# Strassen's seven block products for the second MLP's products with w_a and w_b

## The chip, the cores and the metric

The kernel runs on one core of a Trainium2 chip. The metric is the device time of one execution in microseconds, as the median of several runs. Beside it there is one profiled execution, from which all rows here are taken.

## The reference

Sparse attention (a window and block summaries) makes x of 1536 tokens by 512. Two MLPs follow; the change is in the second one. All data are float32; the weights come in as float64, which the kernel turns to float32 words itself.

```python
h = x @ w_in                        # 512 -> 2048
x = (h * sigmoid(h)) @ w_out        # 2048 -> 512, the y of the kernel
a = x @ w_a                         # 512 -> 1536
b = x @ w_b                         # 512 -> 1536
out = (a * b) @ w_out2              # 1536 -> 512
```

## The kernel before

Every float32 product is made of three passes of TensorE: each operand is split into a high part (a cast to fp32r) and a low part (the rest), and high by high, high by low and low by high are added up in PSUM (`PARTS`). The high part is a copy on ScalarE (ACT), the low part a subtraction on GpSimd (POOL) or VectorE (DVE). A matmul covers 128 rows of the contraction, 128 weight columns and 512 tokens.

A 128x512 piece of weights is loaded as 512 KB of words (`load_words`, L440), decoded by a scaled activation on ACT, a shift (L464) and a join (L468) on DVE, and split (`split`, L493: the high part at L144, the low part on POOL at L491). What is needed for each block of 512 tokens again, w_out and the second MLP's w_out2, is spilled to DRAM as float32 (`spill`) and read back (`reload`).

The first part of the program (attention and the start of the first MLP) is written out as the list `ORDER`. The first MLP then runs in 48 slots, three blocks of 512 tokens by 16 pieces: in slot i the matmuls of `mm1(i)` (L514) and of `mm2(i - 2)` (L545), twelve each. From slot 28 on the loop also loads, decodes and splits one piece of w_a or w_b per slot, which all stay in SBUF.

The last part is the second MLP: 36 jobs, three token blocks by twelve column pieces. In job j `mm34(j, "a")` and `mm34(j, "b")` (L574) make twelve matmuls each into a PSUM bank of their own, two banks each in turn; `chain2(j)` copies a (ACT, L584), multiplies (DVE, L589), takes the high part (ACT, L590) and the low part (DVE, L591); then `mm5(j - 1, t)` adds the job before it to the outputs of four groups of 128 tokens (L601), twelve matmuls. In the first twelve jobs pieces of w_out2 are decoded too.

Every engine works through its instructions in the order in which the program gives them out (`tc.manual_schedule()`), and waits for semaphores at their head. All DMAs go through SP's queue.

Of the kernel before, what the change touches and what calls it, by code (L numbers as in the profile page):

```python
# [18 lines left out]
P = 128  # L19
# [62 lines left out]
def attention_then_two_mlps(ctx, tc, q, k, v, w_in, w_out, w_a, w_b, w_out2, out):  # L82
# [19 lines left out]
    N2 = F2 // P  # L102
    NSTEP = B * NJ
# [18 lines left out]
    boot = ExitStack()  # L122
    ps_b = boot.enter_context(tc.tile_pool(name="ps_b", bufs=1, space=PSUM))
# [316 lines left out]
    def load_words(kind, f, pool):  # L440
        t = pool.tile([P, TB, 2], U32, tag="stage", name=f"st_{kind}{f}", bufs=STAGE_BUFS)
# [9 lines left out]
    def decode_a(kind, f):  # L451
# [3 lines left out]
        w32 = w32_t[kind, f] = work.tile([P, TB], F32, tag="w32", name=f"w32_{kind}{f}", bufs=3)  # L455
# [81 lines left out]
    def mm2(i):  # L537
        n, f = divmod(i, N1)
        g, w = g_t.pop(i), wout_t.pop(i)
        if f == 0:  # L540
            for c in range(NK):
                y_ps[n, c] = pools["y"].tile([P, TB], F32, tag=f"y{c}", name=f"y{n}_{c}", bufs=1)
        for c in range(NK):
            for a, m in PARTS:
                nc.tensor.matmul(y_ps[n, c], w[:, a, c * P:(c + 1) * P], g[:, m, :],  # L545
                                 start=(f == 0 and (a, m) == (0, 0)),
                                 stop=(f == N1 - 1 and (a, m) == PARTS[-1]))
        if f == N1 - 1:
            if n:
                for c in range(NK):  # L550
                    y_high(n, c)
                    y_low(n, c)

    def y_high(n, c):
        if n not in y_t:
            y_t[n] = x_pools[n].tile([P, 2, NK, TB], F32R, tag="xy", name=f"yt{n}", bufs=2 if n < 2 else 1)
        nc.scalar.copy(y_t[n][:, 0, c, :], y_ps[n, c])

    def y_low(n, c):
        y = y_t[n]  # L560
        nc.vector.tensor_tensor(y[:, 1, c, :], y_ps[n, c], y[:, 0, c, :].bitcast(F32), op=ALU.subtract)


    JOBS = NBLK * N2
    wab_t, wo2_t, p_t, ab_ps, o_ps = {}, {}, {}, {}, {}

    def mm34(j, which):
        n, f = divmod(j, N2)
        pool = pools["h"] if which == "a" else pools["g"]
        ps = pool.tile([P, TB], F32, tag="h", name=f"{which}{j}")  # L570
        idx = 0
        for c in range(NK):
            for a, m in PARTS:
                nc.tensor.matmul(ps, wab_t[which, f][:, a, c * P:(c + 1) * P], y_t[n][:, m, c, :],  # L574
                                 start=(idx == 0), stop=(idx == 3 * NK - 1))
                idx += 1
        ab_ps[which, j] = ps

    def chain2(j):

        pa, pb = ab_ps.pop(("a", j)), ab_ps.pop(("b", j))
        sg = work.tile([P, TB], F32, tag="sg", name=f"a_sb{j}")
        g = work.tile([P, 2, TB], F32R, tag="g", name=f"p{j}", bufs=3)
        nc.scalar.copy(sg, pa)  # L584
        parts = 2 if j == JOBS - 1 else 1
        ab = sg if j == JOBS - 1 else pb
        for i in range(parts):
            c = slice(i * TB // parts, (i + 1) * TB // parts)
            nc.vector.tensor_tensor(ab[:, c], pb[:, c], sg[:, c], op=ALU.mult)  # L589
            nc.scalar.copy(g[:, 0, c], ab[:, c])  # L590
            nc.vector.tensor_tensor(g[:, 1, c], ab[:, c], g[:, 0, c].bitcast(F32), op=ALU.subtract)  # L591
        p_t[j] = g

    def mm5(j, t):

        n, f = divmod(j, N2)
        g, w = p_t[j], wo2_t[j]
        if f == 0:
            o_ps[n, t] = pools["y"].tile([P, DM], F32, tag=f"y{t}", name=f"o{n}_{t}", bufs=1)
        for a, m in PARTS:  # L600
            nc.tensor.matmul(o_ps[n, t], g[:, a, t * P:(t + 1) * P], w[:, m],  # L601
                             start=(f == 0 and (a, m) == (0, 0)),
                             stop=(f == N2 - 1 and (a, m) == PARTS[-1]))
        if f == N2 - 1:
# [12 lines left out]
    with tc.manual_schedule():  # L617
# [30 lines left out]
        def end_first():  # L648
            first.close()
            pools["x2"] = x_pools[2] = ctx.enter_context(tc.tile_pool(name="x2", bufs=1, side="right"))  # L650

        def end_att():
            att.close()
            pools["late"] = ctx.enter_context(tc.tile_pool(name="late", bufs=1))
# [23 lines left out]
            "m1": mm1, "sg": silu, "gh": gate_high, "gl": gate_low, "m2": mm2, "yh": y_high, "yl": y_low,  # L678
# [19 lines left out]
        for i in range(att_end + 1, SLOTS):  # L698
# [6 lines left out]
            if i < att_end + 2 * N2:  # L705
                w34(i - att_end, pools["late"])
# [79 lines left out]
```

## Time and profile before

| | |
|---|---|
| Median of 3 runs | 652.96 us (651.45 to 653.8) |
| Profiled execution | 651.7 us, of which the instructions span 650.0 us |
| TensorE's granted clock | 0.999 of full speed |
| PE busy | 632.3 us, 97% of the span |
| DVE, ACT, POOL busy | 314.9, 297.2, 225.4 us |
| Last part (products with w_a, w_b and w_out2) | from 345.77 us to the end |

The engines run side by side, so the busy times don't add up. An engine's busy time tells how much work it has; the chain of waits tells which work the end waits for.

### The profile page before, as it was taken

Reading aid. Unit: us, or ns where it says so; the run is one execution under the profiler, and the core shown is the slowest. Engines: PE = TensorE matmul, PEld = TensorE weight load, DVE = VectorE, ACT = ScalarE, POOL = GpSimd, SP = SyncE. Lnnn points to the kernel's source line nnn. Section 1 sums busy time; section 2 is a strip of 40 time slices with the busy share of each in tenths; the row PEclk is TensorE's granted clock in tenths of the full one; section 3 lists DMA queues with packets and bytes.
Section 4 is the critical chain, followed back from the end, with each engine's and each line's share of the span. In section 5 each row is a group of like instructions: output and inputs, shape, how many; then the busy total and the mean of one; then the engine's idle time right before and its main releaser. Section 6 shows DMA issues by size and latency. Waiting matters only on the chain.

```text
span 650.0 us, 9031 instructions
## 1 busy us (share of the span) xinstructions
PE 632.3 (97%) x3296; PEld 524.2 (81%) x3296; DVE 314.9 (48%) x631; ACT 297.2 (46%) x644; POOL 225.4 (35%) x197
## 2 busy tenths in 40 slices
PE   6899999899999999999999999999999999999997
PEld 5888877788878888888888888888888888888886
DVE  6999878985753244544445664442111112211112
ACT  4999678858655125655555342222222222221112
POOL 5657566553233315455553331111111111111111
PEclk9999999999999999999999999999999999999999
DMA  9898997754121234344453432221311110311101
GB/s 232 182 225 254 287 268 244 200 167 114 47 70 49 59 102 141 131 150 143 145 189 113 172 109 98 97 82 32 114 33 33 33 32 17 113 33 32 33 18 65
DMA packets 80148, 75.72 MB, mean 117 GB/s; under 512 B 37848, under 2 KB 62680, under 8 KB 80104
## 3 DMA queue, kind: packets, MB, share of 16 engines
q1 hardware_dynamic: 80104, 75.15, 39.6%
q8 instruction: 26, 0.43, 0.3%
q14 instruction: 18, 0.15, 0.1%
HBM read 64.36 MB, written 10.49 MB: 115 GB/s over the span
## 4 chain that ended last, share of the span: by engine, by line
PE 83%; ACT 6%; DVE 6%; DMA 2%; issue 2%; SPq 0%; DVEq 0%; ACTq 0%
PE y L545 17%; PE h L514 16%; PE o L601 15%; PE a L574 15%; PE b L574 15%; DMA sp_out<-w_out 2%; PE sc L357 2%; ACT sm L386 1%; PE av L420 1%; PE pt L406 1%; DVE u_in L464 1%; ACT qb L345 1%; DVE w_in L468 1%; DVE raw_q L146 1%; DMA st_q<-in_q_dram 1%
## 5 line engine op out<-in xcount | busy, mean ns | idle before, releaser
L514 PE MATMUL h<-x,w_in 128*128 128x512 f32 (+1 forms) x612 | 142.3, 382 | 0.8 <-DVE g L529 0.6
L545 PE MATMUL y<-g,w_out 128*128 128x512 f32 x576 | 140.9, 394 | 0.7 <-DVE w_out L491 0.7
L491 POOL TENSOR_TENSOR w_out<-re_out,w_out 128x512 fp32r<-128x512 f32 x49 | 68.0, 1389 | 206.0 <-ACT w_out L144 198.7
L514 PEld LDWEIGHTS h<-x,w_in 128*128 128x128 f32 x612 | 108.9, 188 | 22.9 <-issue 0.8
L545 PEld LDWEIGHTS y<-g,w_out 128*128 128x128 f32 x576 | 106.8, 188 | 24.2 <-DVE w_out L491 1.2
L589 DVE TENSOR_TENSOR b<-b,a_sb 128x512 f32<-128x512 f32 x35 | 24.5, 700 | 174.2 <-PE b L574 174.2
L574 PE MATMUL a<-yt,w_a 128*128 128x512 f32 x432 | 104.3, 390 | 0.0
L601 PE MATMUL o<-w_out,p 128*128 128x512 f32 x432 | 104.2, 390 | 0.0
L574 PE MATMUL b<-yt,w_b 128*128 128x512 f32 x432 | 104.1, 390 | 0.0
L601 PEld LDWEIGHTS o<-w_out,p 128*128 128x128 f32 x432 | 81.1, 188 | 17.4
L574 PEld LDWEIGHTS a<-yt,w_a 128*128 128x128 f32 x432 | 81.1, 188 | 17.3
L574 PEld LDWEIGHTS b<-yt,w_b 128*128 128x128 f32 x432 | 81.1, 188 | 17.1
L584 ACT COPY a_sb<-a 128x512 f32<-128x512 f32 x36 | 21.1, 585 | 107.3 <-PE a L574 107.3
L590 ACT CAST p<-b 128x512 fp32r<-128x512 f32 x35 | 20.5, 586 | 101.5 <-DVE b L589 101.5
L491 POOL TENSOR_TENSOR w_out<-w_out,w_out 128x512 fp32r<-128x512 f32 x23 | 30.9, 1343 | 90.2 <-ACT w_out L144 81.7
L529 DVE TENSOR_TENSOR g<-h,g 128x512 fp32r<-128x512 f32 x31 | 21.4, 691 | 66.1 <-ACT g L144 66.0
L529 POOL TENSOR_TENSOR g<-sg,g 128x512 fp32r<-128x512 f32 x17 | 24.4, 1438 | 36.7 <-ACT g L144 13.5
L591 DVE TENSOR_TENSOR p<-b,p 128x512 fp32r<-128x512 f32 x35 | 24.2, 691 | 22.8 <-ACT p L590 22.8
L144 ACT CAST w_out<-re_out 128x512 fp32r<-128x512 f32 x50 | 31.1, 623 | 7.6 <-PE y L545 5.1
L522 ACT ACTIVATE h<-h 128x512 f32<-128x512 f32 x31 | 18.0, 582 | 29.6 <-PE h L514 29.6
L464 DVE TENSOR_SCALAR u_out<-st_out 128x512 uint32<-128x512 uint32 x28 | 29.1, 1044 | 0.0
L386 ACT ACTIVATE sm<-sm,st 128x120 f32<-128x120 f32 x76 | 29.1, 390 | 0.1
(119 smaller groups left out, 706.7 us busy)
## 6 DMA issues: line engine op xcount, KB each, us to landing
st_out<-in_moe_w_out_dram SPq DMA_DIRECT2D x28, 512.0 KB, 4.3
re_out<-sp_out SPq DMA_DIRECT2D x56, 256.0 KB, 2.7
st_in<-in_moe_w_in_dram SPq DMA_DIRECT2D x16, 512.0 KB, 5.8
sp_out<-w_out SPq DMA_DIRECT2D x28, 256.0 KB, 2.3
st_a<-in_moe_w_a_dram SPq DMA_DIRECT2D x12, 512.0 KB, 3.7
st_b<-in_moe_w_b_dram SPq DMA_DIRECT2D x12, 512.0 KB
vw<-in_v_dram SPq DMA_DIRECT2D x20, 192.0 KB, 4.1
vg<-in_v_dram SPq DMA_DIRECT2D x8, 384.0 KB, 5.9
```

The costliest lines, as they stand in the source:

```text
L144: nc.scalar.copy(o, i)
L386: nc.scalar.activation(sm[:, pr, :], sm[:, pr, :], AF.Exp, scale=-1.0, bias=st[:, 0, pr:pr + 1], accum_out=st[:, 1, pr:pr + 1])
L464: nc.vector.tensor_scalar(u, t[:, :, 0], 29, None, op0=ALU.logical_shift_right)
L491: engine.tensor_tensor(w[:, 1], w32_t[kind, f], w[:, 0].bitcast(F32), op=ALU.subtract)
L514: nc.tensor.matmul(h_ps[i][:, cols], win_t[f][:, a, c * P:(c + 1) * P], x_t[n][:, steps, m, c, :], start=(idx == 0), stop=(idx == 3 * NK - 1))
L529: engines[engine].tensor_tensor(g_t[i][:, 1], sg_t.pop(i), g_t[i][:, 0].bitcast(F32), op=ALU.subtract)
L545: nc.tensor.matmul(y_ps[n, c], w[:, a, c * P:(c + 1) * P], g[:, m, :], start=(f == 0 and (a, m) == (0, 0)), stop=(f == N1 - 1 and (a, m) = ...
L574: nc.tensor.matmul(ps, wab_t[which, f][:, a, c * P:(c + 1) * P], y_t[n][:, m, c, :], start=(idx == 0), stop=(idx == 3 * NK - 1))
L584: nc.scalar.copy(sg, pa)
L589: nc.vector.tensor_tensor(ab[:, c], pb[:, c], sg[:, c], op=ALU.mult)
L591: nc.vector.tensor_tensor(g[:, 1, c], ab[:, c], g[:, 0, c].bitcast(F32), op=ALU.subtract)
L601: nc.tensor.matmul(o_ps[n, t], g[:, a, t * P:(t + 1) * P], w[:, m], start=(f == 0 and (a, m) == (0, 0)), stop=(f == N2 - 1 and (a, m) == P ...
```

## The change

Per pair of column pieces (128 columns each of two halves of the 1536) and per half of the contraction (two times 256), the 2x2 block product W^T y is done by a form of Strassen's algorithm with seven block products. The 1536 tokens go in two passes of 768, each in two halves of 384, so that a block of y is 256 by 384. One unit is the a or the b of one pair of column pieces (`KINDS`): even units are a, odd ones b, twelve units a pass. A unit has seven products of six matmuls (two times 128 rows by three parts), on 384 tokens. They go into two PSUM banks, A and B, by turns; several products add to what a bank holds after DVE or ACT has read it, and the four results of a unit are made from the banks and three temporaries (t1, u2, u3). After each product k come a `chunk` on PE (one output step of the pair before: three matmuls of 512 columns, in `mm5`) and `fills` on the other engines.

The fills of unit u prepare the weights of unit u + 1: four additions of 128x256 on DVE make the sums S1 to S4 in `c32`, the seven slots are split in `wab` (high parts on ACT in three pieces; low parts on POOL for slots 0 to 2 and 5 to 6, on DVE for 3 to 4). The weights of w_a and w_b no longer stay split in SBUF: the decoded float32 words are spilled (`spill_u`) and a unit of them, 512 KB, is read back two units ahead (`reload_unit`). y is kept as float32 (`keep_y`), its sums T1 to T4 and its seven operands' splits are made for pass one in slots 35 to 47, for pass two in units 2 to 5 (`sums_again`, POOL) and 11 (`split_again`). Four tiles of w_a and w_b are decoded in units 1, 3, 5 and 7, the pieces of w_out2 in the even units of pass one.

```diff
+    PRODUCTS = ((A11, "B11", 0, False), (S2, "T2", 1, False), (A12, "B21", 0, True), (S3, "T3", 1, True),
+                (S1, "T1", 0, False), (A22, "T4", 1, True), (S4, "B22", 0, True))
...
+    def reload_unit(u):
+        open_unit(u)
+        nc.sync.dma_start(c32_t[u][:, 0:4].rearrange("p b x -> p (b x)"), spill_u[u % UNITS].rearrange("p i x -> p (i x)"))
+
+    def prepare(u):
...
+        def lo(e, lo, hi_):
+            return lambda: engines[e].tensor_tensor(wab_t[u][:, 1, lo:hi_], c32_t[u][:, lo + 1:hi_ + 1],
+                                                    wab_t[u][:, 0, lo:hi_].bitcast(F32), op=ALU.subtract)
+        return [hi(0, 3), add("v", 4, 0, 1, ALU.add), lo("p", 0, 3), add("v", 5, 4, 2, ALU.subtract), hi(3, 5),
+                add("v", 6, 2, 0, ALU.subtract), lo("v", 3, 5), add("v", 7, 3, 5, ALU.subtract), hi(5, 7),
+                lo("p", 5, 7)]
...
+    def group(u, chunks, fills, later):
...
+        done = {2: ((0, 0), A, None), 4: ((1, 1), A, u3), 5: ((1, 0), B, t1), 6: ((0, 1), A, u2)}
+        for k, (s, y, b, more) in enumerate(PRODUCTS):
+            ps = (A, B)[b]
+            idx = 0
+            for c in range(2):
+                for a, m in PARTS:
+                    nc.tensor.matmul(ps, W[:, a, s, c * P:(c + 1) * P], yc_t[y][m][:, c, :], start=(idx == 0 and not more),
+                                     stop=(idx == 5), skip_group_check=more)
+                    idx += 1
+            now, later[:] = list(later), []
+            if k == 0:
+                nc.scalar.copy(t1, A)
+            elif k == 1:
+                nc.vector.tensor_tensor(u2, B, t1, op=ALU.add)
+            elif k == 3:
+                nc.vector.tensor_tensor(u3, B, t1, op=ALU.add)
+            else:
+                (i, t), ps, x = done[k]
+                if w == 0:
+                    a_t[i, t] = temp("a", f"a{p}_{i}{t}", 4)
+                    if x is None:
+                        nc.scalar.copy(a_t[i, t], ps)
+                    else:
+                        nc.vector.tensor_tensor(a_t[i, t], ps, x, op=ALU.add)
+                else:
+                    at = a_t[i, t]
+                    hi, lo = high_low_p(p, i, t, "v" if k in (4, 6) else "p")
+                    if x is None:
+                        nc.vector.tensor_tensor(at, ps, at, op=ALU.mult)
+                    else:
+                        ct = temp("c", f"c{p}_{i}{t}", 2)
+                        nc.vector.tensor_tensor(ct, ps, x, op=ALU.add)
+                        engines["v" if k == 6 else "p"].tensor_tensor(at, ct, at, op=ALU.mult)
+                    later.append(lambda hi=hi, lo=lo: (hi(), later.append(lo)))
+            for f in now:
+                f()
+            for f in chunks[k]:
+                f()
+            for f in fills[k]:
+                f()
...
+            if 0 < u < 2 * UNITS - 1:
+                spread(prepare(u + 1))
+            if w == 0:
+                if p < PAIRS:
+                    spread([lambda: decode("out2", 2 * p, pools["w"]), lambda: decode("out2", 2 * p + 1, pools["w"])], 1, 5)
...
+                fills[0].append(lambda p=p: high_wo2(2 * p))
+                fills[1].append(lambda p=p: low_wo2(2 * p))
+                fills[3].append(lambda p=p: high_wo2(2 * p + 1))
+                fills[4].append(lambda p=p: low_wo2(2 * p + 1))
...
+                n = 4 if p == PAIRS else 6
```

How the change moves the instructions on DVE is seen in one pair of jobs before, here jobs 5 and 6 (b and a_sb are the two products, p the result, u_out2 and w32_out2 the decoder's words).

```order
L589 TENSOR_TENSOR b5_3930<-b5_3930,a_sb5_3943 128x512
L591 TENSOR_TENSOR p5_3944<-b5_3930,p5_3944 128x512
L464 TENSOR_SCALAR u_out26_3969<-st_out26_3908 128x512
L468 SCALAR_TENSOR_TENSOR w32_out26_3966<-w32_out26_3966,u_out26_3969 128x512
L589 TENSOR_TENSOR b6_3986<-b6_3986,a_sb6_3999 128x512
L591 TENSOR_TENSOR p6_4000<-b6_3986,p6_4000 128x512
```

After the change this is the stretch of unit 4, the a of pair 2 in pass one, from its product 1 to its end (bank0 and bank1 are the PSUM banks, c32_5 and wab5 the next unit's weights, a2_.. the unit's results).

```order
L468 TENSOR_SCALAR u_out24_4054<-st_out24_3920 128x512
L472 SCALAR_TENSOR_TENSOR w32_out24_4051<-w32_out24_4051,u_out24_4054 128x512
L628 TENSOR_TENSOR c32_5_3915<-c32_5_3915 128x256
L701 TENSOR_TENSOR u3_4_4020<-bank1_3586,t1_4_4018 128x384
L628 TENSOR_TENSOR c32_5_3915<-c32_5_3915 128x256
L468 TENSOR_SCALAR u_out25_4085<-st_out25_3935 128x512
L472 SCALAR_TENSOR_TENSOR w32_out25_4082<-w32_out25_4082,u_out25_4085 128x512
L709 TENSOR_TENSOR a2_11_4096<-bank0_3585,u3_4_4020 128x384
L638 TENSOR_TENSOR wab5_4036<-c32_5_3915,wab5_4036 128x512
L628 TENSOR_TENSOR c32_5_3915<-c32_5_3915 128x256
L709 TENSOR_TENSOR a2_10_4109<-bank1_3586,t1_4_4018 128x384
L709 TENSOR_TENSOR a2_01_4121<-bank0_3585,u2_4_4019 128x384
```

The decoder's rows now stand between readings of PSUM banks (u3, a2_11, a2_10, a2_01), and additions and a low part of weights stand among them, which before was POOL's.

POOL before has nothing but the low parts of weights, here around the start of the last part.

```order
L491 TENSOR_TENSOR w_out20_3647<-w32_out20_3611,w_out20_3647 128x512
L491 TENSOR_TENSOR w_out21_3693<-w32_out21_3654,w_out21_3693 128x512
L491 TENSOR_TENSOR w_b10_3701<-w32_b10_3696,w_b10_3701 128x512
L491 TENSOR_TENSOR w_out22_3763<-w32_out22_3724,w_out22_3763 128x512
L491 TENSOR_TENSOR w_a11_3771<-w32_a11_3766,w_a11_3771 128x512
```

After the change these are POOL's rows of unit 5, the b of pair 2 in pass one (t32 are sums of y, a2_11 and a2_10 the products a * b, p2_00 a low part for the output product; w_out24 and w_out25 are pieces 4 and 5 of w_out2).

```order
L638 TENSOR_TENSOR wab6_4139<-c32_6_4034,wab6_4139 128x768
L495 TENSOR_TENSOR w_out24_4144<-w32_out24_4051,w_out24_4144 128x512
L655 TENSOR_TENSOR t32_3864<-yt1_2908,t32_3864 128x768
L718 TENSOR_TENSOR a2_11_4096<-c2_11_4203,a2_11_4096 128x384
L675 TENSOR_TENSOR p2_00_4188<-a2_00_4064,p2_00_4188 128x384
L495 TENSOR_TENSOR w_out25_4194<-w32_out25_4082,w_out25_4194 128x512
L718 TENSOR_TENSOR a2_10_4109<-c2_10_4219,a2_10_4109 128x384
L638 TENSOR_TENSOR wab6_4139<-c32_6_4034,wab6_4139 128x512
```

The multiplications, a low part of the product and a sum of y have come into POOL's queue between the low parts of weights.

## Rows read from the trace of the kernel before

**Rows 1.** The page, part 1: busy us, share of the span, instructions by engine.

```profile
PE 632.3 (97%) x3296; PEld 524.2 (81%) x3296; DVE 314.9 (48%) x631; ACT 297.2 (46%) x644; POOL 225.4 (35%) x197
```

**Rows 2.** The chain of waits in order of time, last part: start us, us, what.

```profile
345.77 2.72 PE a L574 x12
...
544.33 2.76 PE a L574 x12
...
640.92 5.50 PE o L601 x24
```

**Rows 3.** Windows of the last part: busy us by engine, clock, DMA.

```profile
345.77:544.33 198.56, 198.56 (x877) 164.47 (x877) 69.72 (x87) 55.26 (x99) 37.52 (x30) 1.00 0.23 77
544.33:650.00 105.67, 102.07 (x444) 83.00 (x443) 19.64 (x31) 22.68 (x41) 16.02 (x13) 0.99 0.14 45
```

**Rows 4.** PE and weight loads by line and form: busy us, mean ns | idle before.

```profile
L574 PE MATMUL a<-yt,w_a 128*128 128x512 f32 x432 | 104.3, 390 | 0.0
L574 PEld LDWEIGHTS a<-yt,w_a 128*128 128x128 f32 x432 | 81.1, 188 | 17.3
```

**Rows 5.** PE in order of time, 46.4 to 48.8 us: start us, us, operation.

```profile
46.21 2.80 PE L514 MATMUL h<-x,w_in 128*128 128x256 f32 x22
```

**Rows 6.** DVE and ACT by line and form, operations of several sizes.

```profile
L589 DVE TENSOR_TENSOR b<-b,a_sb 128x512 f32<-128x512 f32 x35 | 24.5, 700 | 174.2 <-PE b L574 174.2
L491 DVE TENSOR_TENSOR w_out<-re_out,w_out 128x512 fp32r<-128x512 f32 x7 | 4.8, 682 | 0.0
L589 DVE TENSOR_TENSOR a_sb<-b,a_sb 128x256 f32<-128x256 f32 x2 | 0.8, 422 | 6.2 <-PE b L574 6.2
...
L144 ACT CAST w_out<-re_out 128x512 fp32r<-128x512 f32 x50 | 31.1, 623 | 7.6 <-PE y L545 5.1 <-POOL g L529 2.5
L584 ACT COPY a_sb<-a 128x512 f32<-128x512 f32 x36 | 21.1, 585 | 107.3 <-PE a L574 107.3
L590 ACT CAST p<-a_sb 128x256 fp32r<-128x256 f32 x2 | 0.8, 406 | 3.4 <-DVE a_sb L589 3.4
```

**Rows 7.** POOL by line and form.

```profile
L491 POOL TENSOR_TENSOR w_a<-w_a,w_a 128x512 fp32r<-128x512 f32 x12 | 15.6, 1298 | 16.5 <-ACT w_a L144 15.2 <-PE h L514 1.3
L296 POOL TENSOR_TENSOR vg<-vg 96x256 f32<-96x256 f32 x5 | 4.1, 830 | 0.4
```

**Rows 8.** DVE and POOL in order of time, 378 to 386 us.

```profile
380.43 1.29 POOL L491 TENSOR_TENSOR w_out<-w_out,w_out 128x512 fp32r<-128x512 f32 x1 [3.77 <-ACT w_out L144]
380.48 1.53 DVE L464 TENSOR_SCALAR u_b<-st_b 128x512 uint32<-128x512 uint32 x1
...
382.10 0.69 DVE L468 SCALAR_TENSOR_TENSOR w_b<-w_b,u_b 128x512 uint32<-128x512 uint32 x1
382.71 0.42 DVE L464 TENSOR_SCALAR u_out<-st_out 128x512 uint32<-128x512 uint32 x1
...
383.52 1.29 POOL L491 TENSOR_TENSOR w_b<-w_b,w_b 128x512 fp32r<-128x512 f32 x1 [1.80 <-ACT w_b L144]
...
384.05 1.32 DVE L468 SCALAR_TENSOR_TENSOR w_out<-w_out,u_out 128x512 uint32<-128x512 uint32 x1 [0.92 <-ACT w_out L458]
```

**Rows 9.** POOL and DVE in order of time around 56 us.

```profile
53.93 3.16 POOL L491 TENSOR_TENSOR w_in<-w_in,w_in 128x512 fp32r<-128x512 f32 x2
...
56.22 0.67 DVE L529 TENSOR_TENSOR g<-h,g 128x512 fp32r<-128x512 f32 x1
```

**Rows 10.** DVE and POOL in order of time around 117 us.

```profile
116.32 3.85 DVE L296 TENSOR_TENSOR vg<-vg 96x512 f32<-96x512 f32 x3
...
116.87 1.74 POOL L529 TENSOR_TENSOR g<-sg,g 128x512 fp32r<-128x512 f32 x1
```

**Rows 11.** The last job in order of time; in brackets the idle time and its releaser.

```profile
641.01 0.42 DVE L589 TENSOR_TENSOR a_sb<-b,a_sb 128x256 f32<-128x256 f32 x1 [6.24 <-PE b L574]
641.47 0.41 ACT L590 CAST p<-a_sb 128x256 fp32r<-128x256 f32 x1 [2.62 <-DVE a_sb L589]
```

**Rows 12.** DMA issues: what, queue, count, KB each, median us to landing.

```profile
re_out<-sp_out SPq DMA_DIRECT2D x56, 256.0 KB, 2.7
```

More of the change, by code (lines that the diff above doesn't have):

```diff
@@ L440, in load_words @@
     def load_words(kind, f, pool):
[L441 removed]
+        t = pool.tile([P, TB, 2], U32, tag="stage", name=f"st_{kind}{f}", bufs=STAGE_BUFS if pool is decp else 3)
         w = words[kind]
@@ L537, in mm2, with mm2_part @@
     def mm2(i):
+        for c in range(NK):
+            mm2_part(i, c)
+    def mm2_part(i, c):
         n, f = divmod(i, N1)
-        g, w = g_t.pop(i), wout_t.pop(i)
         if f == 0:
[L541 to L561, printed above, removed]
@@ L564, in attention_then_two_mlps @@
[L564 to L592, printed above, removed]
@@ new lines, in mm2_part, with keep_y @@
+        if f == N1 - 1 and n:
+            keep_y(n, c)
+    def keep_y(n, c):
+        lo = n * TB
+        while lo < (n + 1) * TB:
+            q = lo // PT
+            hi = min((n + 1) * TB, (q + 1) * PT)
+            if q not in y_t:
+                y_t[q] = big.tile([P, NK, PT], F32, tag="xy", name=f"yt{q}", bufs=2)
+            o, i = y_t[q][:, c, lo - q * PT:hi - q * PT], y_ps[n, c][:, lo - n * TB:hi - n * TB]
+            if n and (c + lo // PT) % 2:
+                nc.vector.tensor_copy(o, i)
+            else:
+                nc.scalar.copy(o, i)
+            lo = hi
@@ new lines, in mm5 @@
+    def mm5(p, i, t):
+        q, pp = divmod(p, PAIRS)
+        g, w = p_t[p, i, t // 3], wo2_t[2 * p + i]
+        if (q, t) not in o_ps:
+            pool, tag, n = (pools["y"], f"y{t}", 1) if t < 4 else (pools["g"], "h", 2)
+            o_ps[q, t] = pool.tile([P, DM], F32, tag=tag, name=f"o{q}_{t}", bufs=n)
+        begins, ends = (pp == 0 and i == t // 3), (pp == PAIRS - 1 and i != t // 3)
+        for a, m in PARTS:
+            c = (t % 3) * P
+            nc.tensor.matmul(o_ps[q, t], g[:, a, c:c + P], w[:, m], start=(begins and (a, m) == (0, 0)),
+                             stop=(ends and (a, m) == PARTS[-1]))
+        if ends:
+            osb = work.tile([P, DM], F32, tag="w32" if q and t % 2 else "sg", name=f"osb{q}_{t}", bufs=3 if q and t % 2 else 2)
+            ps, r0 = o_ps.pop((q, t)), q * PT + t * P
+            parts = 2 if q and t == PT // P - 1 else 1
@@ L712, in load_wo2 @@
+            steps_y(i)
+        tiles_loaded, tiles_decoded = SLOTS - att_end, SLOTS - att_end - 1
+        last_x.close()
+        pools["post"] = ctx.enter_context(tc.tile_pool(name="post", bufs=1, side="right"))
+        banks += [pools["h"].tile([P, TH], F32, tag="h", name=f"bank{i}") for i in range(2)]
         def load_wo2(j):
             if j < N2:
-                load_words("out2", j, pools["late"])
-            elif j < JOBS:
+                load_words("out2", j, pools["w"])
+            else:
@@ L754, in attention_then_two_mlps, with high_wo2, low_wo2, sums_again @@
-        for j, t in ((2, 0), (2, 1), (2, 2), (1, 0), (1, 1), (1, 2), (2, 3), (1, 3)):
-            mm5(JOBS - j, t)
+        def high_wo2(j):
+            wo2_t[j] = high("out2", j % N2, work, "w2", 3)
+        def low_wo2(j):
+            low("out2", j % N2, wo2_t[j], nc.gpsimd)
+        t32 = {}
+        def sums_again(which):
+            if not t32:
+                t = big.tile([P, 4, 2, TH], F32, tag="xy", name="t32", bufs=2)
+                t32.update({x[0]: t[:, i] for i, x in enumerate(SUMS)})
+            sum_y(1, which, t32, "p")
```

241 lines of the change are left out of this document (164 added, 77 removed).

## The prediction

> **What bounds the kernel now.** I read the page's busy shares first: PE is busy for 632.3 of 650.0 us, no other engine for half [rows 1]. Then the chain of waits, which is where the change lies: from 345.77 us, where the products with w_a and w_b begin, to the last matmul at 646.42 us it is nothing but PE, twelve matmuls every 2.72 us, later 2.76 [rows 2]. That last part is 646.42 - 345.77 = 300.65 us, and the windows say that PE has no idle time in it (the second one's 3.6 us lie behind the last matmul) while DVE works 89.4, ACT 78.0 and POOL 53.5 us [rows 3]. So each matmul column saved counts, as long as the other three engines stay hidden. Most is decided by how much new work they get.
>
> **What PE saves.** A matmul of 512 columns takes 2.72/12 = 226.7 ns [rows 2]. One of 256 columns takes (2.80 - 0.28)/21 = 120 ns from start to start, where 0.28 is the tail of the last one [rows 5]. The 256 columns between them cost 106.7 ns, so 384 columns cost 173.3 ns; a weight load lasts 188 ns [rows 4] but runs under the matmul before it, as the 120 ns show. The change replaces 864 matmuls of 512 columns by 24 units x 7 products x 6 = 1008 of 384. Work of the last part: 1008 x 0.1733 = 174.7, plus 432 of the output product and 24 left of the first MLP at 0.2267 = 103.4: **278.1 us**, 22.6 less than now.
>
> **What the others get.** Prices for the new sizes, between rows [rows 6, 7]: DVE with one input in PSUM 0.56 for 384 elements (0.70 at 512, 0.42 at 256); DVE with both inputs in SBUF 0.41, 0.55, 0.68, 0.95 for 256, 384, 512, 768; ACT 0.48 from PSUM and 0.51 from SBUF at 384, 0.84 at 768; POOL 1.29 at 512 (0.83 at 256), so 1.01 at 384 and 1.84 at 768. The decoder's shift and join are 0.42 and 0.69 alone [rows 8]. Adding up all calls of the new last part gives DVE 173 us, ACT 124, POOL 161: POOL three times what it had. None is over 278, but they are not free of each other.
>
> **The shared port.** At 380.48 us DVE's shift comes 0.05 us after a POOL subtraction began and takes 1.53 us instead of 0.42: it runs only from 381.59, 0.13 us before POOL ends. At 384.05 a join takes 1.32 instead of 0.69, again behind POOL [rows 8]. Three additions on DVE with both inputs in SBUF (some 1.4 us of work) took 3.85 us with POOL busy [rows 10]. A DVE operation that reads PSUM isn't held: 0.67 us at 56.22, in the middle of POOL's work [rows 9]. So DVE's SBUF-only work and POOL's take turns, in the order in which they ask, with 0.13 us of overlap. Today this costs nothing, since DVE waits 174.2/35 = 5 us for PE in each job [rows 6]. After the change DVE also empties the two PSUM banks, and PE waits for that. The Trainium skill (SBUF — State Buffer, section "SBUF: two separate sides") calls this port pair an exclusive lock, held for the whole instruction, and the loser blocks fully. The trace agrees but for the 0.13 us; with none given back the chains below would sum to 51 us of stalls and 682 us, by the row to 32.
>
> For a pair of units (a and b of one pair of blocks) in pass one PE needs 2 x (42 x 0.1733 + 18 x 0.2267) = 22.7 us. POOL has in pairs 1 and 2: 2 x (1.84 + 1.29) for weights, 2 x 1.29 for w_out2, 4 x 1.01 for products, 2 x 1.84 for sums of y = 16.6 us; DVE's SBUF-only part is 8 additions, 2 low parts, 3 decodings and 3 of products = 9.7 us. With 31 turns x 0.13 given back the port needs 22.2 of 22.7 us, and DVE has 11 bank readings of 0.56 in the same queue. In the other pairs of pass one the port needs 17 to 18.
>
> **The chains, worked by hand.** A PSUM result is readable 0.26 us after the point at which the next matmul could start: a matmul's own 390 ns less its pace of 227 [rows 2, 4], and 0.09 from the end at 640.92 to DVE's start at 641.01 [rows 2, 11]. A waiting PE starts 0.15 us after the reader's end, my estimate: 0.05 for the hand-over [rows 11] and 0.1 of a weight load that nothing covers.
>
> *Even units of pass one.* Zero is where POOL starts the low part of weight slots 0 to 2 (1.84 us), about when product 3 starts, since its high part stands behind t1 on ACT. Product 3 ends at 1.03, its bank could be read at 1.29; product 5, which adds to its bank, is due at 1.03 + 0.68 + 1.04 + 0.68 = 3.43. DVE must first do the shift, the join and one addition, then read the bank (u3). The shift waits to 1.71, ends 2.13; POOL takes its next operation, a sum of y (1.84), at 2.00; the join waits to 3.71, ends 4.40; addition 4.81; u3 5.37; product 5 starts at 5.52, 2.1 late. From u3 on DVE alone sets the pace: addition, shift, join, a11, low part, addition, a10 = 3.73 us, then the next unit's first product, at 9.25 instead of 6.19. That is 3.1 us for units 2 and 4. Without the sum (units 6, 8, 10) the join runs at 2.13, u3 ends at 3.80 and 1.5 us are lost. In all five, product 2 also waits 0.45 to 0.5 us for the copy t1: ACT has it behind the high part of p10, which stands behind four POOL operations (1.01 + 1.01 + 1.29 + 1.01). Sum 2 x 3.1 + 3 x 1.5 + 2.4 = **13.0**.
>
> *Odd units of pass one.* Decoding one more weight tile stands ahead of product 2's reading, and POOL's 1.84 ahead of that: 2.1 in unit 1 and 1.3 at its end, 1.2 in units 3 and 5, 0.3 in 7: **6.0**.
>
> *The change of pass.* Unit 11 also splits the seven operands of the next pass: 5.9 us on ACT, 3.8 on DVE, 5.5 on POOL, with products 3 and 5, then output steps 0 and 3 late by 0.9, 0.6, 2.1, 1.7. Units 12 and 13 have four output steps instead of six as cover and lose 0.6, 0.3 and 1.4: **7.5**.
>
> *Pass two* has no decoding and no sums: t1 alone, 0.44 to 0.51 in five units, **2.3**.
>
> *The end.* From the end of product 4 of the last unit: c11 to 0.82, then POOL in a row 1.01, 1.01, 1.29, 1.01 to 5.2, high part 5.8, low part held by DVE to 7.0, second output step at 7.2 instead of 4.1: **3.1**.
>
> Stalls: 13.0 + 6.0 + 7.5 + 2.3 + 3.1 = 31.9 us. Last part: 278.1 + 31.9 + 0.2 drain = 310.2 against 300.65: **+9.5 us**.
>
> **At nothing.** The slots of 257 to 345 us get decoded tiles spilled, sums and splits of y and lose the split of w_a and w_b. Per slot of 5.53 us DVE has at most 4.3 and POOL 3.1 us, a second MLP product trails by two slots, so 5 us late shows nothing; without that cover a slot would lose up to 1 us. Reloading 512 KB a unit (256 KB land in 2.7 us [rows 12], so some 5) is issued a unit of 11 us ahead. SP's spill waits for a join, and behind it stand loads needed a unit later. The four low parts of y dropped from the attention part lay under a busy PE. If the 2.76 us pace of [rows 2] came up for all matmuls, PE's work would be 4.4 us more, of which the stalls swallow 2.5.
>
> **Bounds.** With POOL's prices 10% down or up the chains give 25 or 42 us of stalls, 655 or 672 us.
>
> **Rivals.** *Faster.* DVE isn't held as often as I reckon: in [rows 6] seven low parts on DVE average 682 ns, no wait at all. Without any port wait the same chains leave 9.2 us (change of pass 3.7, end 2.9): 278.1 + 9.4 - 300.65 = -13.2, 640 us. It decides once stalls are below 22.6. I give 0.15 to nearly that, and 0.10 to something between, 643 to 651. *No change*, 651 to 655: stalls of 20.5 to 24.5, which happen to eat the saving; 0.10. *Worse*, over 672: POOL slower than priced, no overlap of the port's turns, or weight loads of 188 ns binding the 173 ns matmuls (1008 x 15 ns = 15 us), against which the 120 ns speak; 0.08. *The forecast*, 655 to 672: 0.57.
>
> **The numbers.** The profiled execution took 651.7 us, 1.3 under the median of 652.96; I add the 9.5 us to the median: **662 us**. From the cases: faster by over 0.3% (2 us, about what a measurement here tells from no change) 0.25, within it 0.10, slower 0.65. The range leaves out the fastest 0.12 and the 0.08 over 672: 643 to 672; that of the likeliest alone is 655 to 672.
>
> **What would show it.** PE's spacing 173 ns in the new line and 278 us of work in the last part; PE idle some 30 us there, named after DVE's bank readings; DVE's additions, shifts and joins of the new last part far above 0.41, 0.42 and 0.69 on average; the first pass some 161 us long up to the second's first product, the second 149, though it has 5 us more PE work. I am wrong if DVE's SBUF-only operations run at their lone durations beside a busy POOL, or if PE idles under 20 us.

## The result and the profile after

The changed kernel takes 658.40 us (median of 4 runs, 658.32 to 658.66), the kernel before beside it 652.28 us (4 runs, 651.45 to 653.8): ratio 1.0092, interval 1.007 to 1.0113. The change costs 6.1 us. The forecast was 9.5 us more, with 655 to 672 us as the likeliest case.

The page of the changed kernel, its busy shares:

```profile
PE 625.6 (95%) x3440; PEld 537.1 (82%) x3440; DVE 479.4 (73%) x851; ACT 327.9 (50%) x703; POOL 338.1 (51%) x267
```

PE has less to do than in [rows 1] and the span is longer all the same: 656.6 us (the execution 658.35). DVE and POOL went up by 164.5 and 112.7 us. The first matmul of the last part starts at 347.16 us, the last ends at 652.88: 305.7 us against 300.65 before by [rows 2], so 5.1 of the 6.6 us between the two profiled spans. ([rows 2] counts from the end of the matmul ahead; from the first start, 345.60, to the last end, 646.40, it was 300.8, which makes it 4.9.) The windows of its two passes (units 0 to 11, units 12 to 23 with the end) answer to [rows 3]:

```profile
347.16:503.94 156.78, 146.69 (x721) 126.86 (x720) 135.18 (x179) 61.54 (x112) 95.59 (x64) 1.00 0.35 123
503.94:656.60 152.66, 146.12 (x745) 132.99 (x743) 103.86 (x148) 51.27 (x95) 85.89 (x61) 1.00 0.22 73
```

Columns: length, then PE, weight loads, DVE, ACT, POOL, clock, DMA share, GB/s. PE isn't gapless any more, and the view of waits says who it waits for: what, for whom, us in all, times, longest.

```profile
PE bank L692 <- DVE u L701: 4.5, 6, 1.7
PE bank L692 <- DVE c L717: 2.1, 3, 1.0
PE o L737 <- POOL p L675: 1.6, 2, 1.1
PE o L737 <- ACT p L672: 1.3, 1, 1.3
PE o L737 <- DVE p L675: 1.2, 1, 1.2
PE bank L692 <- DVE a L714: 0.9, 1, 0.9
PE bank L692 <- DVE u L699: 0.8, 2, 0.5
```

Two thirds of it are DVE's readings of the two PSUM banks. The worst place, in order of time (start us, us, what): product 5 of unit 2, which waits for u3 (L701).

```profile
375.85 0.91 DVE L675 TENSOR_TENSOR p<-a,p 128x384 fp32r<-128x384 f32 x1
...
376.31 2.16 POOL L638 TENSOR_TENSOR wab<-c,wab 128x768 fp32r<-128x768 f32 x1
...
376.68 2.07 DVE L468 TENSOR_SCALAR u_out<-st_out 128x512 uint32<-128x512 uint32 x1
...
378.43 2.01 POOL L655 TENSOR_TENSOR t<-yt 128x768 f32<-128x768 f32 x1
378.84 2.15 DVE L472 SCALAR_TENSOR_TENSOR w_out<-w_out,u_out 128x512 uint32<-128x512 uint32 x1
...
380.92 0.41 DVE L628 TENSOR_TENSOR c<-c 128x256 f32<-128x256 f32 x1
...
381.25 0.55 DVE L701 TENSOR_TENSOR u<-bank,t 128x384 f32<-128x384 f32 x1
...
381.85 0.44 PE L692 MATMUL bank<-yh0T,wab 128*128 128x384 f32 x1 [1.74 <-DVE u L701]
```

The shift has 0.42 us of work and takes 2.07: it ends 0.28 us after POOL's low part. The join has 0.69 and takes 2.15, behind POOL's sum. Only then come one addition and the reading, while the bank has been ready since product 3. This is the chain of the forecast, operation by operation. The reading itself isn't held: all 132 readings of the two banks by DVE in the last part take 0.54 to 0.56 us, whatever POOL does meanwhile. (That the shift begins its own 0.42 us 0.14 us before POOL ends at 378.47 is where the rows differ from the Trainium skill, SBUF — State Buffer, section "SBUF: two separate sides", by which the lock is held for the whole instruction.)

From here on a **stall** is what the start of a matmul comes later than the line's pace after the start of the one before (0.176 us after a matmul of 384 columns, 0.233 after one of 512), over all 1464 matmuls of the last part from the trace's starts. (Counted are starts over 50 ns late.) It is more than PE's idle time by busy shares, some 13 us, since a matmul's modelled end lies some 0.16 us behind the point at which the next could start.

### The profile page after: what moved, and what is told of

It reads as the page before. It is cut to its first block, busy times and chain, and to the rows that moved or that the text cites. A ratio compares the mean times of both kernels' runs of the same rounds, so it can differ in the third digit from the quotient of the medians.

```text
span 656.6 us, 9756 instructions
## 1 busy us (share of the span) xinstructions
PE 625.6 (95%) x3440; PEld 537.1 (82%) x3440; DVE 479.4 (73%) x851; ACT 327.9 (50%) x703; POOL 338.1 (51%) x267
## 5 line engine op out<-in xcount | busy, mean ns | idle before, releaser
L638 POOL TENSOR_TENSOR wab<-c,wab 128x768 fp32r<-128x768 f32 (+1 forms) x48 | 83.4, 1738 | 77.6 <-ACT wab L634 77.6
L634 ACT CAST wab<-c 128x512 fp32r<-128x512 f32 (+1 forms) x72 | 49.6, 691 | 87.0 <-DVE c L628 87.0
L628 DVE TENSOR_TENSOR c<-c 128x256 f32<-128x256 f32 x96 | 82.8, 864 | 0.0
L692 PE MATMUL bank<-yh0T,wab 128*128 128x384 f32 x192 | 58.0, 343 | 6.1 <-DVE u L701 4.5
L692 PE MATMUL bank<-yh1T,wab 128*128 128x384 f32 x192 | 56.7, 337 | 0.0
L672 ACT CAST p<-a 128x384 fp32r<-128x384 f32 x48 | 24.5, 513 | 63.6 <-POOL a L718 60.5
L718 POOL TENSOR_TENSOR a<-c,a 128x384 f32<-128x384 f32 x24 | 31.5, 1314 | 35.1 <-DVE c L717 35.1
L692 PEld LDWEIGHTS bank<-yh0T,wab 128*128 128x128 f32 x192 | 35.5, 188 | 12.6 <-DVE u L701 7.9
L692 PE MATMUL bank<-yh0B,wab 128*128 128x384 f32 x144 | 44.0, 349 | 1.7 <-DVE c L717 1.1
L533 POOL TENSOR_TENSOR g<-sg,g 128x512 fp32r<-128x512 f32 x17 | 24.2, 1421 | 36.2 <-ACT g L147 13.1
L692 PE MATMUL bank<-yh1B,wab 128*128 128x384 f32 x144 | 41.5, 339 | 1.0 <-DVE c L717 1.0
L692 PEld LDWEIGHTS bank<-yh1T,wab 128*128 128x128 f32 x192 | 35.5, 188 | 2.2
```

The costliest lines, as they stand in the source:

```text
L533: engines[engine].tensor_tensor(g_t[i][:, 1], sg_t.pop(i), g_t[i][:, 0].bitcast(F32), op=ALU.subtract)
L628: return lambda: engines[e].tensor_tensor(o, x, y, op=op)
L634: nc.scalar.copy(wab_t[u][:, 0, lo:hi_], c32_t[u][:, lo + 1:hi_ + 1])
L638: return lambda: engines[e].tensor_tensor(wab_t[u][:, 1, lo:hi_], c32_t[u][:, lo + 1:hi_ + 1], wab_t[u][:, 0, lo:hi_].bitcast(F32), op=ALU ...
L672: nc.scalar.copy(p_t[p, i, t][:, 0], a_t[i, t])
L692: nc.tensor.matmul(ps, W[:, a, s, c * P:(c + 1) * P], yc_t[y][m][:, c, :], start=(idx == 0 and not more), stop=(idx == 5), skip_group_chec ...
```

## The experiments

All are edits of the changed kernel. Executions of one kernel differ by up to 4 us (648.26 to 652.16 in combination 2), and the granted clock has a part in it (below), so stalls and work of the last part are compared, in us, and times are given beside them. Experiments 1 to 8 were executed once each. What an edit doesn't touch repeats closely: units 11 to 14 have 6.0 to 6.3 us of stalls in the changed kernel and in experiments 2, 3 and 7.

| | forecast | after | lows kept | sums odd | decode late | pairs | no split | combo 2 | combo 3 |
|---|---|---|---|---|---|---|---|---|---|
| unit 0 | 0 | 0.4 | 0.4 | 0.4 | 0.4 | 0.4 | 0.4 | 0.4 | 0.1 |
| units 2, 4, ... 10 | 13.0 | 9.4 | 1.4 | 5.3 | 2.0 | 10.4 | 9.3 | 4.0 | 1.5 |
| units 1, 3, ... 9 | 6.0 | 3.7 | 1.6 | 5.6 | 6.1 | 3.3 | 3.7 | 1.7 | 0.2 |
| units 11 to 14 | 7.5 | 6.1 | 6.3 | 6.1 | 6.0 | 6.0 | 2.7 | 6.1 | 5.7 |
| units 15 to 22 | 2.3 | 0 | 0 | 0 | 0 | 0 | 0 | 0.2 | 0.1 |
| unit 23 and the end | 3.1 | 2.3 | 2.3 | 3.9 | 3.9 | 3.9 | 3.9 | 3.9 | 1.3 |
| stalls | 31.9 | 21.9 | 12.0 | 21.2 | 18.3 | 23.9 | 20.0 | 16.3 | 8.8 |
| PE's work | 278.1 | 283.8 | 283.7 | 283.8 | 283.9 | 281.8 | 283.9 | 281.6 | 281.5 |

A wait at a unit's first product stands with that unit; the forecast counted it with the unit before, and unit 14's wait for t1 with pass two. In its count the changed kernel has 9.3, 4.2, 5.5 and 0.3 in rows two to five.

The 3.9 us at the end are 2.3 us and a fallen clock: behind PE's two waits there (1.5 and 0.65 us) the next eight starts come 0.19 us late each, the 1.2 GHz level. The windows of "decode late", same columns as above:

```profile
636.00:640.00 4.00, 2.20 (x10) 1.29 (x9) 3.10 (x4) 0.93 (x2) 3.20 (x3) 1.00 0.00 0
640.00:644.00 4.00, 4.00 (x11) 3.17 (x12) 0.93 (x2) 0.58 (x1) 0.00 (x0) 0.57 0.18 66
```

The changed kernel's own profiled run had the same waits and kept the clock. So 1.5 us of those columns is no effect of the edits.

**1. POOL's weight low parts left out (lows kept).**

```diff
+            if e == "p" and u > 1:
+                return lambda: None
-            return lambda: engines[e].tensor_tensor(wab_t[u][:, 1, lo:hi_], c32_t[u][:, lo + 1:hi_ + 1],
+            return lambda: engines[e].tensor_tensor(wlo[u % 2][:, lo:hi_], c32_t[u][:, lo + 1:hi_ + 1],
...
```

> Leaves out POOL's low parts of the weights from unit 2 on (five of seven slots keep those of the first two units), 44 subtractions of 1.84 and 1.29 us, some 70 us of POOL's work; DVE's work and its queue stay as they are. If the stalls come from the port that DVE's SBUF-only operations share with POOL, the stalls of the last part fall from 21.9 us to some 9 (what is left is the change of pass and the end) and the span from 656.6 to about 644; the additions of the weights on DVE fall from 864 to some 500 ns on average. If DVE's queue is simply too long between two bank readings, DVE's own load is unchanged and the stalls stay above 18 us, the span above 653. The products' pace of 176.5 ns should stay by both.

Measured: 647.58 us, span 645.9, stalls 12.0; those of units 2 to 10 fall from 11.3 to 2.4. DVE's work and queue are unchanged, but its additions are held far less. DVE by line, after (first) and here (the same lines, with their numbers moved by up to five): busy us, mean ns.

```profile
L628 DVE TENSOR_TENSOR c<-c 128x256 f32<-128x256 f32 x88 | 79.6, 905 | 0.0
...
L468 DVE TENSOR_SCALAR u_out<-st_out 128x512 uint32<-128x512 uint32 x12 | 13.3, 1107 | 0.8 <-DMA st_out<-in_moe_w_out_dram 0.8
...
L701 DVE TENSOR_TENSOR u<-bank,t 128x384 f32<-128x384 f32 x24 | 13.2, 549 | 4.3 <-PE bank L692 4.3
```

```profile
L629 DVE TENSOR_TENSOR c<-c 128x256 f32<-128x256 f32 x88 | 47.1, 535 | 0.0
...
L706 DVE TENSOR_TENSOR u<-bank,t 128x384 f32<-128x384 f32 x24 | 13.3, 555 | 18.3 <-PE bank L697 18.3
...
L468 DVE TENSOR_SCALAR u_out<-st_out 128x512 uint32<-128x512 uint32 x12 | 8.3, 695 | 0.8 <-DMA st_out<-in_moe_w_out_dram 0.8
```

The port theory holds, with 9.9 us of stalls gone for POOL work alone; a DVE queue that is too long by itself is out. A shorter POOL queue could also help by giving its results sooner, but the view of waits shows DVE waiting for no result of POOL in the last part of either kernel, and only 0.6 of the 9.9 us were waits for t1, ACT's copy. So what POOL costs there lies inside DVE's operations. The change of pass and the end stayed at 6.3 and 2.3, as expected; that the total is 12.0 and not 9 comes from 3.4 us left in units 0 to 5.

**2. The sums of y in the odd units.**

```diff
-            if 2 <= u < 6:
-                fills[3].append(lambda i=u - 2: sums_again(i))
+            if u in (3, 5, 7, 9):
+                fills[0].append(lambda i=(3, 5, 7, 9).index(u): sums_again(i))
```

> The four sums of y (POOL, 2.0 to 2.3 us each) move from units 2 to 5 to the odd units 3, 5, 7 and 9. By the port theory units 2 and 4 lose only what unit 6 does now, 1.3 us instead of 3.6 and 3.0, and the odd units, where the port has slack, at most 0.5 more each: span 656.6 down by 2 to 4 us, to 653 or 654. If what counts is only the sum of the port's work in pass one, nothing changes: 656 to 657.

Measured: 656.50 us, span 654.8. Units 2 and 4 go from 3.6 and 3.0 to 2.2 and 0.8, units 3, 5 and 7 from 0.6, 0.6 and 0.4 to 1.1: 2.3 us net in pass one. Place counts, not only the port's sum.

**3. Decoding after products 4 and 5.**

```diff
-  ... decode("out2", 2 * p + 1, pools["w"])], 1, 5)
+  ... decode("out2", 2 * p + 1, pools["w"])], 4, 6)
```

> In the even units of pass one the two decodings of w_out2 (shift and join on DVE) come after products 4 and 5 instead of 1 and 3; work on every engine is the same. If PE waits because its bank readings stand in DVE's queue behind operations held by POOL, product 5 of units 2 and 4 no longer waits 1.9 us nor that of 6, 8 and 10 0.5 us; some of it comes back at the next unit's first product: 3 to 5 us less, span about 652. If the port is full whatever the order, the wait only moves: 656 to 657.

Measured: 654.25 us, span 652.5. Product 5 waits nowhere in units 1 to 10; even units 9.4 to 2.0, odd ones 3.7 to 6.1, 5.0 us net. Same work, other order in DVE's queue: PE waits because the bank reading stands behind operations that POOL holds.

**4. Output steps in pairs.**

```diff
-                    chunks[k].append(rest.pop(0))
+                    chunks[k // 2 * 2].append(rest.pop(0))
```

> Two output steps stand together after products 0, 2 and 4 instead of one after each of the first six, so there are 66 fewer switches between the 384-column products and the 512-column output steps. In the trace of after, the six products behind an output step take 1062 ns and three output matmuls 698, where six products behind other products take 1040: some 40 ns a switch. By this theory a unit of pass two without stalls falls from 11.59 to about 11.47 us, the last part's work from 283.9 to about 281.2 us; the waits may grow by 0 to 2 us for less cover between products 1 and 3. The rival, that a matmul's pace doesn't depend on its neighbours, gives 11.59 us again.

PE of the changed kernel (first) and here, in order of time, a product behind an output step and, here, one behind another product:

```profile
573.66 0.86 PE L737 MATMUL o<-w_out,p 128*128 128x512 f32 x3
574.35 0.33 PE L692 MATMUL bank<-yh1T,wab 128*128 128x384 f32 x1
...
575.42 0.86 PE L737 MATMUL o<-w_out,p 128*128 128x512 f32 x3
```

```profile
562.03 1.55 PE L737 MATMUL o<-w_out,p 128*128 128x512 f32 x6
563.41 0.33 PE L692 MATMUL bank<-yh1T,wab 128*128 128x384 f32 x1
...
564.46 0.33 PE L692 MATMUL bank<-yh1B,wab 128*128 128x384 f32 x1
...
565.50 1.32 PE L737 MATMUL o<-w_out,p 128*128 128x512 f32 x5
```

Six products behind an output step take 1.07 (after) and 1.05 us (here), behind another product 1.04, the forecast's pace; three output matmuls 0.69, or 1.38 for six. A unit of pass two falls from 11.59 us (mean of 11.60 and 11.58) to 11.50 (11.54 and 11.46), PE's work from 283.8 to 281.8. That is 30 ns for each of the 66 places saved, most of it in the products (176.2 to 174.5 ns on average; output matmuls 232.4 to 231.5). The time was 659.25 us: stalls grew by 2.0 us, 1.6 of them the fallen clock at the end and most of the rest lost cover, and the last part starts 0.9 us later, which the edit doesn't reach. Why a switch costs this I can't say.

**5. Two output steps held back in units 11 and 23.**

```diff
-                    chunks[k].append(rest.pop(0))
+                    chunks[6 if k > 3 and u in (UNITS - 1, 2 * UNITS - 1) else k].append(rest.pop(0))
```

> In units 11 and 23 the output steps that stood after products 4 and 5 come after product 6, in front of the steps that wait. In the changed kernel PE waits 1.2 and 1.45 us there in unit 11 and 1.5 and 0.65 us in unit 23; two steps are 1.4 us of work. If these waits are only for other engines' chains, most of 1.4 us comes back at each place, less what products 5 and 6 of unit 11 lose for want of cover: stalls 21.9 down to 19.5 to 20.5, span some 655 with TensorE's clock at full speed throughout. The rival: the chains behind the last products start later by as much, since they hang on PE's last product of the unit, which doesn't move: no, product 6 itself ends 1.4 us sooner. So a result of no gain would speak for chains that hang on POOL and not on product 6.

Measured: 657.57 us, stalls 21.9, no gain, a miss. In unit 11 the wait ahead of the first step fell from 1.2 to 0.6 us, but product 5 waits 1.0 instead of 0.3; the second stays at 1.45. In unit 23 the first wait grew from 1.5 to 1.85 us. So the chain there doesn't hang on PE's product 6, as the expectation had it for this result, and PE merely waits elsewhere.

**6. The splits of the change of pass left out (no split).**

```diff
-            if u == UNITS - 1:
-                for k, x in enumerate(PRODUCTS):
-                    fills[k].append(lambda y=x[1], k=k: split_again(y, "p" if k % 2 else "v"))
```

> Leaves out the splits of the seven operands of y at the change of pass (7 copies on ACT, 4 subtractions on DVE, 3 on POOL, all in unit 11): pass two works on the operands of pass one again. If the port is what the change of pass waits for, the stalls of units 11 to 14 fall from 6.1 us to 2 or less, span 656.6 to 652. If they hang on the chain behind unit 11's last products (addition, product, high part, low part, then four output steps at once), which stays, the wait of 1.2 and 1.45 us ahead of the output steps stays and at least 3.5 us of the 6.1 are left. Nothing else should move.

Unit 11 with four output steps, windows of after (first) and here:

```profile
485.54:503.94 18.40, 15.66 (x72) 12.81 (x73) 14.48 (x17) 9.64 (x17) 15.63 (x10) 1.00 0.19 57
```

```profile
485.10:500.06 14.96, 14.76 (x72) 13.10 (x73) 10.07 (x15) 4.97 (x10) 10.24 (x8) 1.00 0.21 70
```

Unit 11's stalls go from 4.1 to 0.7 us, units 11 to 14 from 6.1 to 2.7; the time was 656.09 us with the fallen clock at the end. That lies between the two expectations (2 or less, or at least 3.5 left). So most of unit 11's stalls are the splits', 4.4 us less work on DVE, 5.4 on POOL and 4.7 on ACT, and the chain behind the last products alone costs 0.4. Which of the three engines counts isn't separated by this edit. The rows of the changed kernel show two of them: POOL's product starts at 497.28 behind its split of 495.41 (1.90 us), and the last two bank readings, from 500.63, behind DVE's split of 498.94 (1.76 us). The 1.5 us of unit 14 stayed. Most of them are its first product at 525.84: the bank reading that it waits for (525.14, 0.55 us) stands behind an addition of 0.41 us of work that takes 1.23 beside POOL's product (523.56, 1.39 us), and unit 13 has only four output steps as cover.

**7. DVE instead of POOL in the last pair.**

```diff
-                    hi, lo = high_low_p(p, i, t, "v" if k in (4, 6) else "p")
+                    hi, lo = high_low_p(p, i, t, "v" if k in (4, 6) or p == 2 * PAIRS - 1 else "p")
-                        engines["v" if k == 6 else "p"].tensor_tensor(at, ct, at, op=ALU.mult)
+                        engines["v" if k == 6 or p == 2 * PAIRS - 1 else "p"].tensor_tensor(at, ct, at, op=ALU.mult)
```

> In the last pair (units 22 and 23) the two products and the two low parts of POOL go to DVE, which has 0.55 us for each instead of 1.01 to 1.3. The stall ahead of the last output steps, 2.3 us, should fall to about 1 us by the chain: three POOL operations in a row shorter by 0.6 each; units 22 and 23 have 11.6 us of PE for DVE's 7 to 8, so no new stall. Span 656.6 to 655.4, if the clock holds. If what the end waits for is the port, DVE's operations wait for POOL's last low part of the weights, which is long done there: no difference to the chain.

Measured: 656.22 us, span 654.5; the stall at the end falls from 2.3 to 1.3 us, as expected.

**8. All decoding of pass one moved into the slots of the first MLP.** Slots 29 to 44 decode one more piece each; w_out2 is reloaded in pass one too.

```diff
+            if d + 1 in extra:
+                extra[d + 1][0]()
             decode_tile(d, d < 4)
+            if d in extra:
+                extra[d][1]()
...
```

> The decodings of pass one (four tiles of w_a and w_b, twelve pieces of w_out2) move into slots 29 to 44 of the first MLP, one more per slot, and w_out2 is reloaded in pass one as in pass two; the work of all engines is the same, 16 times 1.1 us of DVE in another place. By the port theory the stalls of pass one, 13.1 us with units 0 to 10, fall to some 3 to 5 (the sums of y and POOL's weights are left); the slots, where PE had work without a gap, lose 0 to 3 us. Span 656.6 down to 647 to 650. If instead what pass one loses hangs on the reading of the banks alone, which stays, the stalls of pass one remain above 9 us and the span above 653.

Measured: 664.98 us. In units 1 to 10 the stalls fell from 13.1 to 2.2 us, a little below the 3 to 5 expected, but the last part starts at 360.61, 13.5 us later than in the changed kernel, and unit 0 loses 5.0. That it would cost 0 to 3 us was wrong. Waits in the slots (all engines):

```profile
DVE w_b L472 <- ACT w_b L462: 15.5, 6, 4.3
...
DVE w_a L472 <- ACT w_a L462: 9.2, 7, 2.4
...
PE h L518 <- DVE g L533: 8.7, 4, 4.5
ACT w_a L462 <- DMA spu<-w_a: 8.5, 3, 4.9
ACT w_b L462 <- DMA spu<-w_b: 8.0, 2, 4.2
```

ACT's decoding waits for the spill that frees its buffer (three `w32` for decoding and reloading), DVE's join for ACT, and behind it in DVE's queue stands the g that PE needs. The DMA engines are busy 0.82 there, against 0.60 in the changed kernel.

**9. Combinations.** Combo 1: the sums in units 3, 5, 7 and 9 (after product 1), decoding late, output steps in pairs, two steps held back in the last unit, and six steps in units 12 and 13 instead of four with four more at the end of unit 11. Combo 2: without the last two. Combo 3: combo 2 with the edit of 7, and with the four tiles and four pieces of w_out2 decoded in every second slot, eight instead of the sixteen of 8.

> The sums of y in units 3, 5, 7 and 9 (after product 1), decoding in the even units after products 4 and 5, output steps in pairs, six instead of four output steps in units 12 and 13 (none right at the end of unit 11), and in the last unit two of them behind product 6. By the port theory, added from the single runs: sums 2.3, decoding 5.1, pairs 2.0 of work less 0.4, the change of pass 1 to 2, the end 1: 10 to 12 us less than the changed kernel, some 646 to 649 us beside 651 to 653 of before. If the gains are the same slack counted twice, only some 5 us: 653.

> The combination before this one without its changes at the change of pass and at the end: sums in the odd units, decoding after products 4 and 5, output steps in pairs, four output steps at the end of unit 11 as in the changed kernel. The combination before lost 5.2 us at the first product of unit 12 and let the clock fall there; with the four steps as cover, units 11 to 14 should take the 6.0 us of stalls of the single runs instead of 8.0, and the last part some 296.5 instead of 298.4 us: 647.5 to 650 us. If the wait only moves back in front of the output steps with the same sum, 650 again.

> The same, and the four tiles of w_a and w_b of units 1 to 7 and four of the twelve pieces of w_out2 are decoded in every second slot of 30 to 44, and the end's low parts and products are DVE's. Units 0 to 3 lose some 2 us less, the end 1 us less; the slots, with every second one holding two decodings, lose nothing if it was the number of decodings in a row that cost 14 us with sixteen of them, and 2 to 6 us if any slot with two decodings is too long: 645 to 648 us by the first, 650 or more by the second.

| | us (median) | ratio to before, interval | last part |
|---|---|---|---|
| combo 1 | 650.44 | 0.9972 (0.9959 to 0.9984) | 298.4 |
| combo 2 | 649.63 | 0.9945 (0.9926 to 0.9964) | 297.8 |
| combo 3 | 642.32 | 0.9827 (0.98 to 0.9854) | 290.4 |

The ratios are against 13 runs of the kernel before (median 653.44, beside which the changed kernel's 658.40 would be 5.0 more). Combo 1 missed its 646 to 649 us, combo 2 came out in its 647.5 to 650, and combo 3 fell below its 645 to 648. Combo 1 lost 5.2 us at unit 12 (3.8 at its first product, the rest at the lower clock); combo 2 avoided that but paid 1.5 us of clock at the end, so 297.8 instead of the expected 296.5. Combo 3 beats both kernels; its stalls are 7.5 us below combo 2's, 2.4 of them in units 4, 6 and 8, which I hadn't expected to gain, and 1.5 by the clock that held at the end. Its slots up to 345 us, its two passes, and all that PE still waits for in the last part:

```profile
257.00:345.00 88.00, 88.00 (x383) 71.72 (x382) 57.88 (x82) 49.41 (x87) 36.05 (x24) 1.00 0.74 248
345.55:489.44 143.89, 140.06 (x722) 127.56 (x720) 113.58 (x162) 57.43 (x104) 95.89 (x64) 1.00 0.30 101
489.44:639.70 150.26, 144.76 (x745) 132.04 (x743) 101.50 (x152) 51.34 (x95) 81.69 (x57) 1.00 0.23 74
```

```profile
PE o L737 <- DVE p L675: 1.9, 2, 1.2
PE o L737 <- POOL p L675: 1.7, 1, 1.7
PE bank L692 <- DVE c L717: 1.6, 2, 0.9
```

The slots stay gapless with eight more decodings. POOL has as much to do in pass one as in the changed kernel (95.89 against 95.59 us), but DVE is busy for 113.58 instead of 135.18: eight decodings are gone from its queue, and less of what is left is held. Combo 3 gains by moved work and by order; the runs don't divide the two.

## Why the forecast was right, point by point

**The sign and the mechanism: right.** PE's work fell by 300.65 - 283.8 = 16.8 us, stalls of 21.9 us took more than that: 5.1 us. But the margin is partly luck. By the forecast's own break-even, 22.6 us of stalls, 21.9 would have been its "no change" rival (20.5 to 24.5), even with the 2.5 us of stalls that slower matmuls may have taken off; the change is clearly slower only because PE saved 5.7 us less than forecast, which moved the break-even to 16.8. The "faster" rival, that DVE is hardly held, falls with experiment 1: without 70 us of POOL's work the same kernel runs in 647.58 us.

**PE's pace: 5.7 us too low.** The term was 1008 x 173.3 + 456 x 226.7 ns. Measured are 176.2 and 232.4 ns on average, without the stalls. The 173 ns are there, but only where a product follows a product; the forecast took the paces of long equal runs and applied them to a stream that switches after every six products. Pairs gave 2.0 of it back. The loads of 188 ns didn't bind the matmuls.

**The stalls: 10 us too high, by one chain after another.** Chain for chain the forecast stood: unit 2 lost 2.0 us at product 5 (forecast 2.1), 0.2 at product 6 and 0.3 at the next first product (together 1.0). What it oversized are the short waits. The copy t1 was to cost 0.44 to 0.51 us in ten units: it cost 0.3 in units 2, 4, 6 and 14 and nothing in 8, 10 and 16 to 22. In the rows of unit 16 there t1 ends at 552.76 and product 2 starts on time at 552.93. A bank was read 0.19 us after the point at which the next matmul could start (546.11, where that was 545.92) instead of 0.26; the 0.15 us after the reader's end held (0.05, then 0.1 at the second matmul). Slower products also leave the others more time: the forecast put 2.5 us on that for 4.4 us more of work. The rest is tenths in some thirty waits, which I didn't separate.

**By part:** even units 13.0 forecast, 9.3 measured in the same count; odd units 6.0 and 4.2; change of pass 7.5 and 5.5; pass two 2.3 and 0.3; end 3.1 and 2.3. First pass 156.8 us instead of 161. The second's 148.9 against 149 is a cancellation too: slower matmuls against fewer stalls.

**At nothing: right in the profile.** PE has 88.00 us of work in the 88 us from 257 to 345. The 1.4 us by which the last part starts later (1.6 by the matmuls' own starts) come from 120 to 128 us, where the granted clock is 0.75 and 0.82 behind a wait of 1.88 us that the kernel before has too, there at 1.00:

```profile
120.00:124.00 4.00, 3.38 (x15) 2.92 (x16) 3.85 (x9) 3.95 (x13) 1.17 (x2) 0.75 0.83 257
124.00:128.00 4.00, 4.00 (x22) 3.40 (x22) 3.77 (x14) 2.49 (x5) 1.38 (x1) 0.82 0.68 182
```

Six of the eleven edited kernels, whose code there is the same, kept 1.00 in this place, five fell as here. So it isn't the change's own, though it stands in its profiled 658.35.

**The tests named beforehand:** additions at 905 ns instead of 410 and the shift at 1107 instead of 420 say port; PE's idle time of 13 us by its busy share would say "wrong" by the words of the forecast (under 20). It had summed delays of starts, which are 21.9 us, and named them idle time.

**The two misses cancel in part:** work 5.7 us too low, stalls 10.0 too high, 4.3 us net, and 1.4 us of clock against it.

## What to carry to other kernels

Fewer TensorE columns are worth only what the other engines leave: before trading matmuls for additions, add up the time that VectorE's SBUF-only work and GpSimd's take as if in one queue, and look for the PSUM readings that stand behind them. Order is as good as work: moving decodings behind the last bank reading of a unit gained 5 us with no instruction less. A combination of such moves, with eight decodings put where the engines had room and some of GpSimd's work on VectorE, turned 6 us lost into 11 gained, with the same algorithm.

## What the runs showed of the hardware that I had not expected

- A matmul's spacing depends on its neighbours: behind three of 512 columns, six of 384 start 168, 178, 185, 176, 181 and 174 ns apart (medians of units 15 to 22), then 173; three output matmuls take 229, 233 and 236 ns, where [rows 2] has 226.7 in a run of equal ones.
- POOL pays for the port too: of its 24 subtractions of weights with 768 columns half take 1.84 to 1.86 us and half 2.16 to 2.29, the sums 2.01 to 2.29. The one of 376.31 shown above took 2.16: it ends 1.71 us after DVE's low part of 375.85 did (376.76), that is its own 1.84 less the 0.13 of overlap.
- Short waits can cost twice: PE waits of 1.5 and 1.9 us were followed by the 1.2 GHz level in some executions and not in others of the same stretch of code, 1.5 us at the end and 1.6 us near 120 us.
